# A state-space layer gated by a GLU: two full-row phases per chunk instead of three, and row statistics of the last chunk on ScalarE

## The chip, the cores and the metric

The kernel runs on one core of a Trainium2 chip. A core has a matrix engine (TensorE, "PE", with its weight loads listed as "PEld"), a vector engine (VectorE, "DVE"), an activation engine (ScalarE, "ACT"), a general engine (GpSimd, "POOL") and a queue that issues transfers (SyncE, "SP"). Each works through its own list of instructions in order and waits for the others by semaphores. The metric is the device time of one execution in microseconds. Beside it there is one profiled execution, whose trace has the start, the length and the releaser of every instruction.

## What is computed

The input `x` has 2048 rows (tokens) of 448 values. Each row is normalized; a diagonal complex recurrence runs along the rows; a gated two-layer network runs on each row; the two are multiplied and added to the input.

```python
x = A_x
xn = _layernorm(x, axis=-1)
s = _A_ref(xn, ...)            # recurrence with 448 complex states, then 2*Re(C h) + xn*Dskip
g = _silu(_B_ref(xn, ...))     # (sigmoid(xn w_gate) * (xn w_up)) w_down, 448 -> 1792 -> 448
return x + s * g

# inside _A_ref
Bu = jnp.einsum("bld,pd->blp", x + 0j, B_bar)
for t in range(L):
    h = Lam_bar[None, :] * h + Bu[:, t, :]
y = 2.0 * jnp.einsum("blp,dp->bld", hseq, Cmat).real + x * Dskip[None, None, :]
```

## The kernel before

The 2048 rows are cut into four chunks of 512 (`L`), and each chunk into four tiles of 128 rows. All matrix products of a chunk use `xnT`, the normalized rows transposed. The work of a chunk is:

- `stats` (line 421): mean and variance of one row tile, a `bn_stats` (L423) and a `bn_aggr` (L424) on DVE. `chain` (line 426) makes from them the factor and the offset of the normalization; for chunks 2 and 3 these are five small POOL instructions on two row tiles at a time (L437 to L446).
- `prepare(c)` (line 508): `norm` writes the normalized tile `xn` with one ACT pass (L456), POOL completes it (L459), two DMA transposes from SP's queue (L373) write it into `xnT`, and `skip_row` multiplies it by `Dskip` on DVE (L464). The `xnT` of chunk 2 lies on the memory of the raw C matrices, so that its transposes must stand behind `c_scale` (line 648), which makes the scaled C matrices `cT` from them (L656, L659, L666, L668).
- `gu_step(c, i)` (line 711): fourteen of them per chunk, seven column blocks, each a gate and an up product. A step is seven pairs of matmuls that use 64 rows of the array each, side by side (L690, L691); I call them half-row pairs. The gate's step is finished by a tanh pass on ACT (L704), the up step by a DVE instruction that writes `hF` (L707). The products use three PSUM buffers `gu`.
- `b_units(c, pts)` (line 733): the input of the recurrence, two of four column groups per call. It starts with half-row pairs (L743 to L748); the rest are full-row matmuls (L758, L761). Between the two the call can put other work (`mid`). ACT copies the result to `bus`.
- `whole(c)` (line 913): the recurrence of the chunk on DVE, three calls of `ssm_pair` and one of `ssm_stack`: rotate (L805, L806, L808), scan (L812, L844), rotate back into `hT` (L826, L827, L829). `hT` has two buffers, for even and odd chunks.
- `down(c, j)` (line 866): 14 full-row matmuls of one row tile (L873), followed by a silu pass on ACT into a buffer `g_t` (L879). `yout(c, j)` (line 884): 7 full-row matmuls with `cT` (L898), then three DVE instructions that add the skip row, multiply with `g_t` and add `x` (L904, L906, L908), and a store from SP (L910). Both take turns on two PSUM buffers `acc`.

The order is not written out engine by engine. The kernel adds operations with their inputs, outputs and an assumed cost to a plan (`Plan.add`, line 85). `Plan.solve` (line 138) keeps PE in the order in which its operations were added, works back from PE's times to the latest time of every other operation, and then lets each other engine take, among the operations that are ready, the one that is due first. So the end of the file, with its calls of `gu_step`, `b_units`, `down` and `yout`, is PE's order, and the lists of DVE, ACT, POOL and SP follow from it and from the assumed costs.

In chunks 1, 2 and 3 PE's order has three stretches of full-row work each: one that opens with `b_units(c, (0, 1))`, one with `b_units(c, (2, 3))`, and one of two `down` and two `yout` before the last two `gu_step`. Behind chunk 3 there is one more, up to the end. `down(c, ...)` runs in chunk c+1, and so do the first two `yout(c, ...)`; the last two run in chunk c+2.

Of the kernel before, what the change touches and what calls it, by code (L numbers as in the profile page):

```python
# [10 lines left out]
FP32 = mybir.dt.float32  # L11
BF16 = mybir.dt.bfloat16
I32 = mybir.dt.int32
ALU = mybir.AluOpType
ACT = mybir.ActivationFunctionType
# [3 lines left out]
D = 448  # L19
# [4 lines left out]
NT = S_TOK // P  # L24
# [4 lines left out]
EPS = 1e-5  # L29
# [44 lines left out]
class Plan:  # L74
# [10 lines left out]
    def add(self, eng, cost, fn, r=(), w=(), dma=0, lat=None, chain=False, name="", rate=230e3):  # L85
        o = Op()
        o.idx, o.eng, o.cost, o.fn, o.dma, o.name = len(self.ops), eng, cost, fn, dma, name
        o.lat = LAT.get(eng, 0.0) if lat is None else lat
        o.pre, o.suc, o.rate = {}, [], rate
        o.slot = None  # L90
        if dma and eng != "POOL":
            o.slot, self.n_dma = self.n_dma, self.n_dma + 1
        o.start = o.end = None
        for k in r:
            if k in self.w:
                self._edge(self.w[k], o, True)
        for k in w:
            for q in self.r.get(k, ()):
                self._edge(q, o, False)
            if k in self.w:  # L100
                self._edge(self.w[k], o, True)
        for k in w:
            self.w[k] = o
            self.r[k] = []
        for k in r:
            if k not in w:
                self.r.setdefault(k, []).append(o)
        if chain or eng == "PE" or (eng == "DVE" and self.seq):
            key = ("chain", eng)
            if key in self.last_of:  # L110
                self._edge(self.last_of[key], o, None)
            self.last_of[key] = o
        self.ops.append(o)
        return o
# [131 lines left out]
def kernel(  # L246
# [18 lines left out]
    V, A, G, T, Q = nc.vector, nc.scalar, nc.gpsimd, nc.tensor, nc.sync  # L265
# [5 lines left out]
    def sbt(name, shape, dt=BF16):  # L271
        return sb.tile([P] + list(shape), dt, name=name)
# [9 lines left out]
    x_all = sbt("x_all", [NT, D])  # L282
# [24 lines left out]
    iota = wv_raw[0][:].bitcast(FP32)  # L307
    NSIG = 2
    sig = [sbt(f"sig{i}", [2, L], FP32) for i in range(NSIG)]
    NGT, NO = 6, 3  # L310
    g_t = [sbt(f"g_t{i}", [D]) for i in range(NGT)]
    o_t = [sbt(f"o_t{i}", [D]) for i in range(NO)]
    ctmp = [sbt(f"ctmp{i}", [D], FP32) for i in range(2)]
# [8 lines left out]
    mv = sbt("mv", [NT, 2])  # L322
# [2 lines left out]
    veb = sbt("veb", [NT, 1])  # L325
    halfc, negc, expc = (sbt(n, [1], FP32) for n in ("halfc", "negc", "expc"))
    sdb = sbt("sdb", [NT, 1])
    rsd = sbt("rsd", [NT, 1], FP32)
    nmr = sbt("nmr", [NT, 1], FP32)
    col = {}  # L330
# [14 lines left out]
    add = pl.add  # L345
# [75 lines left out]
    def stats(t):  # L421
        b = t % 3
        add("DVE", 0.6, lambda: V.bn_stats(out=bst[b][:], in_=x_all[:, t, :]), r=[("x", t)], w=[("bst", b)])  # L423
        add("DVE", 0.16, lambda: V.bn_aggr(out=mv[:, t, :], in_=bst[b][:]), r=[("bst", b)], w=[("mv", t)])  # L424

    def chain(t0, n):
        ts = range(t0, t0 + n)
        var, mean = mv[:, t0:t0 + n, 1:2], mv[:, t0:t0 + n, 0:1]
        sd, rs, nm, ve = (q[:, t0:t0 + n, :] for q in (sdb, rsd, nmr, veb))
        ks = lambda k: [(k, t) for t in ts]  # L430
        if t0 < TPC:
            add("ACT", 0.3, lambda: A.activation(sd, var, ACT.Sqrt, bias=epsc[:]), r=ks("mv") + ["sqrttab", "epsc"], w=ks("sd"))
            add("POOL", 0.15, lambda: G.tensor_copy(out=meanf[:, t0:t0 + n, :], in_=mean), r=ks("mv"), w=ks("mf"))
            add("DVE", 0.2, lambda: V.reciprocal(out=rs, in_=sd), r=ks("sd"), w=ks("rs"))
            return
        bc = lambda t: t[:].unsqueeze(1).to_broadcast((P, n, 1))
        add("POOL", 0.4, lambda: G.tensor_single_scalar(out=ve, in_=var, scalar=EPS, op=ALU.add), r=ks("mv"), w=ks("ve"))  # L437
        add("POOL", 1.0, lambda: G.tensor_tensor(out=sd, in0=ve, in1=bc(halfc), op=ALU.pow), r=ks("ve") + ["consts"], w=ks("sd"))
        if t0 == TPC:
            add("DVE", 0.2, lambda: V.reciprocal(out=rs, in_=sd), r=ks("sd"), w=ks("rs"))  # L440
            add("DVE", 0.16, lambda: V.scalar_tensor_tensor(out=nm, in0=mean, scalar=-1.0, in1=rs, op0=ALU.mult, op1=ALU.mult),
                r=ks("mv") + ks("rs"), w=ks("nm"))
            return
        add("POOL", 1.0, lambda: G.tensor_tensor(out=rs, in0=sd, in1=bc(negc), op=ALU.pow), r=ks("sd") + ["consts"], w=ks("rs"))
        add("POOL", 0.4, lambda: G.tensor_tensor(out=nm, in0=mean, in1=rs, op=ALU.mult), r=ks("mv") + ks("rs"), w=ks("nm"))
        add("POOL", 0.4, lambda: G.tensor_single_scalar(out=nm, in_=nm, scalar=-1.0, op=ALU.mult), r=ks("nm"), w=ks("nm"))  # L446
# [58 lines left out]
    def gate(keys, key):  # L505
        add("NONE", 0.0, lambda: None, w=list(keys) + (key if isinstance(key, list) else [key]), lat=0.0)

    def prepare(c):
        if c == 2:
            gate([("rC", 0), ("rC", 1), ("rC3", 0), ("rC3", 1), "rC3l"], "xnT2free")  # L510
        for j in range(TPC):
            norm(c * TPC + j)
            dma_transpose(c * TPC + j)
            skip_row(c * TPC + j)
# [196 lines left out]
    def gu_step(c, i, first=False):  # L711
        m, k = (i // 2, "gu"[i % 2]) if c else (i % 7, "gu"[i // 7])
        a = next_gu()
        gu_mm(c, k, m, a, 0, TPC, first)
        gu_evac(c, k, m, a)
# [150 lines left out]
    def down(c, j, first=False, bank=None):  # L866
        key, d = bank if bank else (lambda a: (("acc", a), acc[a][:, 0:D]))(next_acc())
        js = slice(j * P, j * P + P)

        def f():  # L870
            for ft in range(FT):
                m, h = ft % 7, ft // 7
                T.matmul(d, lhsT=hF[c % 2][:, m, h, js], rhs=wd[:, ft, :], start=(ft == 0), stop=(ft == FT - 1))  # L873
        add("PE", 14 * 0.189 + (SW if first else 0), f, r=[("wd", 0), ("wd", 1)] + [("hF", c % 2, m) for m in range(7)], w=[key],
            name=f"d{c}.{j}")
        g = gt_n[0] % NGT
        gt_n[0] += 1
        gt_of[c, j] = g
        add("ACT", act(448), lambda: A.activation(g_t[g][:], d, ACT.Silu, scale=0.5), r=[key, "silutab"], w=[("gt", g)])  # L879
# [33 lines left out]
    def whole(c):  # L913
        if c < 2:
            gate([("nu" if c else "v", p) for p in range(4)], [("hT", c, p) for p in range(4)])
        for p in (0, 1):
            ssm_pair(c, p)
        ssm_stack(c)
        ssm_pair(c, 2)
# [31 lines left out]
    load_wd(0)  # L951
    def stats_for(c):
        for t in range(4 * c, 4 * c + 4):
            stats(t)
            if c > 1 and t % 2:
                chain(t - 1, 2)
        if c == 1:
            chain(4, 4)
# [23 lines left out]
    one(1, 0, "u")  # L982
    prepare(2)
    b_units(1, (0, 1), lambda: down(0, 0, True))
    for i in range(3, 6):
        gu_step(1, i, i == 3)
    b_units(1, (2, 3), lambda: down(0, 1, True))
    for i in range(6, 12):
        gu_step(1, i, i == 6)
    down(0, 2, True)  # L990
    yout(0, 0)
    down(0, 3)
    yout(0, 1)
    for i in range(12, 14):
        gu_step(1, i, i == 12)
    whole(1)

    for i in range(0, 4):
        gu_step(2, i)
    b_units(2, (0, 1), lambda: down(1, 0, True))  # L1000
    yout(0, 2)
    for i in range(4, 7):
        gu_step(2, i, i == 4)
    b_units(2, (2, 3), lambda: down(1, 1, True))
    yout(0, 3)
    prepare(3)
    for i in range(7, 12):
        gu_step(2, i, i == 7)
    down(1, 2, True)
    yout(1, 0)  # L1010
    down(1, 3)
    yout(1, 1)
    for i in range(12, 14):
        gu_step(2, i, i == 12)
    whole(2)

    for i in range(0, 4):
        gu_step(3, i)
    b_units(3, (0, 1), lambda: down(2, 0, True))
    yout(1, 2)  # L1020
    for i in range(4, 7):
        gu_step(3, i, i == 4)
    b_units(3, (2, 3), lambda: down(2, 1, True))
    yout(1, 3)
    for i in range(7, 12):
        gu_step(3, i, i == 7)
    down(2, 2, True)
    yout(2, 0)
    down(2, 3)
    yout(2, 1)  # L1030
    for i in range(12, 14):
        gu_step(3, i, i == 12)
    whole(3)

    yout(2, 2, True)
    yout(2, 3)
    free_banks = []
    for s in range(3):
        a = (gu_n[0] + s) % 3
        for i in range(2):  # L1040
            free_banks.append((("gub", a, i), gu[a][:, i, 0:D]))
        gate([("gu", a)], [("gub", a, 0), ("gub", a, 1)])
    for j in range(2):
        down(3, j, bank=free_banks[j])
    for j in range(2):
        yout(3, j)
    down(3, 2, bank=free_banks[2])
    yout(3, 2)
    down(3, 3, bank=free_banks[3])
    a = next_acc()  # L1050
    yout(3, 3, banks=[(("acc", a), acc[a]), free_banks[4]], parts=((0, 128), (128, 448)))
# [36 lines left out]
```

## Time and profile before

| | |
|---|---|
| median of 4 runs | 188.83 us (187.81 to 189.45) |
| profiled execution | 188.76 us |
| its span, first to last instruction | 186.9 us |
| granted clock of TensorE | 0.998 |
| DVE: `bn_stats` (L423), `bn_aggr` (L424) | 16 each, 613 and 166 ns |
| ACT: silu into `g_t` (L879), normalization (L456) | 540 and 755 ns |
| full-row matmuls of `down` and `yout` on 128x448 | 189 ns apart |
| half-row pairs on 512 columns | 215 ns apart |

The span is what the trace shows; the 1.9 us up to the time of the same execution lie around it. Durations of matmuls in the trace are longer than the distance of their starts, since they overlap in the array; the distance is what a matmul costs. A row of a group gives busy time, mean length and the idle time before it. The busy share of an engine is an average over stages with different limits.

### The profile page before, as it was taken

How to read it: one execution, taken by the hardware profiler on the slowest of the kernel's cores; microseconds unless marked ns; L12 is line 12 of the kernel's file. 1: busy time of each engine (PE TensorE's matmuls, PEld its weight loads, DVE VectorE, ACT ScalarE, POOL GpSimd, SP SyncE). 2: the span in 40 equal slices, each digit the busy share in tenths (PEclk: the TensorE clock that was granted, in tenths of full speed). 3: DMA queues.
4: the chain of work that ended last, by engine and by line, in shares of the span. 5: the costliest groups of instructions: out<-in, count | busy, mean ns of one | idle time of the engine just before them, and what ended most of it. 6: DMA issues, size and time to landing. Idle time of an engine off the chain costs nothing.

```text
span 186.9 us, 3512 instructions
## 1 busy us (share of the span) xinstructions
PE 180.4 (96%) x1375; PEld 87.7 (47%) x1375; DVE 167.9 (90%) x303; ACT 88.0 (47%) x124; POOL 35.0 (19%) x87
## 2 busy tenths in 40 slices
PE   7999998999999999999999999999999999999991
PEld 2584443474444444444445445444445445445550
DVE  3832999999998899999999999999999999999963
ACT  3549997953949942241567441324444421501020
POOL 7134351920078100000037410000000000000000
PEclk9999999999999999999999999999999999999999
DMA  5999999399100035200000343000000000001220
GB/s 133 278 213 229 186 212 171 75 263 232 61 4 0 0 76 65 59 0 4 0 2 0 77 102 70 0 28 0 25 4 0 25 25 28 0 2 51 74 77 25
DMA packets 30257, 13.43 MB, mean 72 GB/s; under 512 B 19744, under 2 KB 30240, under 8 KB 30240
## 3 DMA queue, kind: packets, MB, share of 16 engines
q1 hardware_dynamic: 28336, 12.05, 31.0%
q10 hardware_dynamic: 1808, 1.15, 2.3%
q8 instruction: 11, 0.18, 0.4%
q14 instruction: 6, 0.05, 0.1%
q0 software_dynamic: 96, 0.00, 0.0%
HBM read 6.77 MB, written 1.84 MB: 46 GB/s over the span
## 4 chain that ended last, share of the span: by engine, by line
PE 60%; DVE 21%; DMA 8%; ACT 4%; issue 3%; POOL 1%; SPq 1%; DVEq 0%
PE gu L690 24%; PE acc L873 13%; PE acc L898 10%; PE gu L873 6%; DMA x_all<-in_A_x_dram 5%; DVE hF L707 4%; PE gu L758 4%; DMA wG<-in_B_w_gate_dram 3%; DVE wv L812 3%; DVE bst L423 2%; DVE cT L659 1%; DVE ta L805 1%; DVE ta L826 1%; SPq L351 1%; DVE tb L806 1%
## 5 line engine op out<-in xcount | busy, mean ns | idle before, releaser
L690 PE MATMUL gu<-xnT,wG 64*128 64x512 bf16 (+1 forms) x231 | 46.2, 344 | 0.3 <-DVE xnT L491 0.3
L691 PE MATMUL gu<-xnT,wG 64*128 64x512 bf16 (+1 forms) x231 | 46.2, 344 | 0.0
L690 PE MATMUL gu<-xnT,wU 64*128 64x512 bf16 x196 | 46.0, 376 | 0.0
L691 PE MATMUL gu<-xnT,wU 64*128 64x512 bf16 x196 | 46.0, 376 | 0.0
L704 ACT ACTIVATE sig<-gu 128x1024 f32<-128x1024 f32 x21 | 21.4, 1024 | 28.6 <-PE gu L691 24.2
L873 PE MATMUL acc<-wd,hF 128*128 128x448 bf16 x168 | 33.8, 353 | 0.2 <-ACT g_t L879 0.2
L873 PEld LDWEIGHTS <-hF 128*128 128x128 bf16 x224 | 21.2, 98 | 22.6 <-issue 3.9
L690 PEld LDWEIGHTS <-wG 64*128 64x128 bf16 x231 | 21.0, 94 | 21.3 <-issue 2.1
L690 PEld LDWEIGHTS <-wU 64*128 64x128 bf16 x196 | 18.1, 94 | 23.3 <-issue 1.4
L707 DVE SCALAR_TENSOR_TENSOR hF<-sig,gu 128x1024 bf16<-128x1024 f32 x21 | 25.5, 1212 | 2.5 <-PE gu L691 1.3
L812 DVE TENSOR_TENSOR_SCAN wv<-c_r,st,z 128x512 bf16<-128x512 f32 x18 | 23.0, 1275 | 0.0
L898 PE MATMUL acc<-cT,hT 128*128 128x448 bf16 (+1 forms) x112 | 22.6, 344 | 0.0
L691 PEld LDWEIGHTS <-wG 64*128 64x128 bf16 x231 | 20.9, 94 | 0.0
L879 ACT ACTIVATE g_t<-acc 128x448 bf16<-128x448 f32 x12 | 6.5, 540 | 28.5 <-PE acc L873 28.5
L691 PEld LDWEIGHTS <-wU 64*128 64x128 bf16 x196 | 18.1, 94 | 0.1
L758 PE MATMUL gu<-xnT,bT 128*128 128x512 bf16 x72 | 16.9, 379 | 0.0
L423 DVE BATCH_NORM_STATS2 bst<-x_all 128x6 f32<-128x448 bf16 x16 | 9.4, 613 | 7.8 <-DMA x_all<-in_A_x_dram 7.8
L898 PEld LDWEIGHTS <-hT 128*128 128x128 bf16 x119 | 11.3, 98 | 10.0 <-issue 0.4
L769 ACT CAST bus<-gu 128x1024 bf16<-128x1024 f32 x12 | 12.0, 1004 | 2.9 <-PE gu L758 2.8
L456 ACT ACTIVATE xn<-x_all,nmr,rsd 128x448 bf16<-128x448 bf16 x12 | 8.8, 755 | 7.3 <-DVE xd L464 4.6
L873 PE MATMUL gu<-wd,hF 128*128 128x448 bf16 x56 | 11.1, 352 | 0.0
L904 DVE TENSOR_TENSOR o_t<-acc,xd 128x448 bf16<-128x448 f32 (+1 forms) x16 | 9.5, 594 | 1.5 <-PE acc L898 1.4
(135 smaller groups left out, 239.3 us busy)
## 6 DMA issues: line engine op xcount, KB each, us to landing
out_dram<-o_t SPq DMA_DIRECT2D x15, 112.0 KB, 1.7
wd<-in_B_w_down_dram SPq DMA_DIRECT2D x2, 784.0 KB, 5.1
x_all<-in_A_x_dram SPq DMA_DIRECT2D x3, 448.0 KB, 4.8
wU<-in_B_w_up_dram SPq DMA_DIRECT2D x2, 448.0 KB, 11.6
wU<-in_B_w_up_dram SPq DMA_DIRECT2D x2, 336.0 KB, 6.9
wG<-in_B_w_gate_dram SPq DMA_DIRECT2D x2, 224.0 KB, 5.9
wG<-in_B_w_gate_dram ACTq DMA_DIRECT2D x2, 224.0 KB, 5.9
xnT<-xn SPq DMA_TRANSPOSE x24, 2.4
```

What stands on the lines that cost most here:

```text
L423: add("DVE", 0.6, lambda: V.bn_stats(out=bst[b][:], in_=x_all[:, t, :]), r=[("x", t)], w=[("bst", b)])
L456: add("ACT", 0.65, lambda: A.activation(xn[b][:, 0:448], x_all[:, t, :], ACT.Identity, bias=nmr[:, t, :], scale=rsd[:, t, :]), r=[("x", t) ...
L690: T.matmul(gu[a][:, 0, ts], lhsT=w_[0:H, s, ms], rhs=x[0:H, s, ts], start=(s == 0), stop=(s == 6))
L691: T.matmul(gu[a][:, 1, ts], lhsT=w_[H:P, (s + 1) % 7, ms], rhs=x[H:P, s, ts], start=(s == 0), stop=(s == 6))
L704: add("ACT", act(1024), lambda: A.activation(th, gu[a][:], ACT.Tanh, scale=0.5), r=[("gu", a)], w=[tk])
L707: add("DVE", dve1(1024), lambda: V.scalar_tensor_tensor(out=ho, in0=th, scalar=1.0, in1=gu[a][:], op0=ALU.add, op1=ALU.mult), r=[("gu", a) ...
L758: T.matmul(gu[a][:, i, :], lhsT=bT[:, kt, i, pt * P:pt * P + P], rhs=x[:, 2 * kt, :], start=False, stop=(kt == 2))
L769: add("ACT", act(1024), lambda u=u, a=a: A.copy(out=bus[u][:], in_=gu[a][:]), r=[("gu", a)], w=[("bus", u)])
L812: dve(1.194, lambda k=k: V.tensor_tensor_scan(out=wv[:, k, :], data0=rb, data1=z[:, k, :], initial=(st[pt][:, k, :] if c else 0.0), op0=AL ...
L873: T.matmul(d, lhsT=hF[c % 2][:, m, h, js], rhs=wd[:, ft, :], start=(ft == 0), stop=(ft == FT - 1))
L898: T.matmul(y, lhsT=hT[c % 2][:, hm, js], rhs=cT[:, cm, c0:c1], start=(i == 0), stop=(i == 6))
L904: add("DVE", dve1(n), lambda od=od, y=y, c0=c0, c1=c1: V.tensor_tensor(out=od, in0=y, in1=xq[:, c0:c1], op=ALU.add), r=[key, ("xd", q)], w ...
```

## The change

Three things change. The calls at the end of the file are put in another order: each of chunks 1, 2 and 3 has two full-row stretches, each with two `down` and, in chunks 2 and 3, two `yout`, all four of which now belong to chunk c-2; the tail has four `yout(2, ...)` in place of two, and its own order. The mean and the variance of the four row tiles of chunk 3 come from ACT: one Identity pass whose accumulated output is the row's sum, then one Square pass, with minus the mean as its bias, whose accumulated output is the sum of squares; three POOL instructions per two tiles scale them. And there are small edits: one `g_t` buffer fewer, four new small tiles, and higher assumed costs for two POOL operations in `chain`, which the planner uses.

```diff
-    NGT, NO = 6, 3
+    NGT, NO = 5, 3
...
+    junk = sbt("junk", [D])
+    smf, nmf, sqf = (sbt(n, [NT, 1], FP32) for n in ("smf", "nmf", "sqf"))
...
+    def act_stats(t0):
+        sm, nf, sq, me, va = (q[:, t0:t0 + 2, :] for q in (smf, nmf, sqf, mv[:, :, 0:1], mv[:, :, 1:2]))
+        ts = (t0, t0 + 1)
+        for t in ts:
+            add("ACT", 0.62, lambda t=t: A.activation(junk[:], x_all[:, t, :], ACT.Identity, accum_out=smf[:, t, :]),
+                r=[("x", t), "silutab"], w=[("sm", t), "junk"])
+        add("POOL", 0.4, lambda: G.tensor_single_scalar(out=nf, in_=sm, scalar=-1.0 / D, op=ALU.mult),
+            r=[("sm", t) for t in ts], w=[("nf", t) for t in ts])
+        add("POOL", 0.4, lambda: G.tensor_single_scalar(out=me, in_=sm, scalar=1.0 / D, op=ALU.mult),
+            r=[("sm", t) for t in ts], w=[("me", t) for t in ts])
+        for t in ts:
+            add("ACT", 0.62, lambda t=t: A.activation(junk[:], x_all[:, t, :], ACT.Square, bias=nmf[:, t, :],
+                                                      accum_out=sqf[:, t, :]),
+                r=[("x", t), ("nf", t)], w=[("sq", t), "junk"])
+        add("POOL", 0.4, lambda: G.tensor_single_scalar(out=va, in_=sq, scalar=1.0 / D, op=ALU.mult),
+            r=[("sq", t) for t in ts] + [("me", t) for t in ts], w=[("mv", t) for t in ts])
...
-        add("POOL", 0.4, lambda: G.tensor_single_scalar(out=ve, in_=var, scalar=EPS, op=ALU.add), r=ks("mv"), w=ks("ve"))
-        add("POOL", 1.0, lambda: G.tensor_tensor(out=sd, in0=ve, in1=bc(halfc), op=ALU.pow), r=ks("ve") + ["consts"], w=ks("sd"))
+        add("POOL", 0.6, lambda: G.tensor_single_scalar(out=ve, in_=var, scalar=EPS, op=ALU.add), r=ks("mv"), w=ks("ve"))
+        add("POOL", 1.4 if n == 4 else 1.0, lambda: G.tensor_tensor(out=sd, in0=ve, in1=bc(halfc), op=ALU.pow), r=ks("ve") + ["consts"], w=ks("sd"))
...
     def stats_for(c):
         for t in range(4 * c, 4 * c + 4):
-            stats(t)
+            if c not in (3,):
+                stats(t)
+            elif t % 2:
+                act_stats(t - 1)
...
     b_units(1, (0, 1), lambda: down(0, 0, True))
+    down(0, 1)
     for i in range(3, 6):
         gu_step(1, i, i == 3)
-    b_units(1, (2, 3), lambda: down(0, 1, True))
-    for i in range(6, 12):
+    b_units(1, (2, 3), lambda: down(0, 2, True))
+    down(0, 3)
+    for i in range(6, 14):
         gu_step(1, i, i == 6)
-    down(0, 2, True)
-    yout(0, 0)
-    down(0, 3)
-    yout(0, 1)
-    for i in range(12, 14):
-        gu_step(1, i, i == 12)
     whole(1)
...
+    for c in (2, 3):
+        for i in range(0, 4):
+            gu_step(c, i)
+        b_units(c, (0, 1), lambda: down(c - 1, 0, True))
+        yout(c - 2, 0)
+        down(c - 1, 1)
+        yout(c - 2, 1)
+        for i in range(4, 7):
+            gu_step(c, i, i == 4)
+        b_units(c, (2, 3), lambda: down(c - 1, 2, True))
+        yout(c - 2, 2)
+        down(c - 1, 3)
+        yout(c - 2, 3)
+        if c == 2:
+            prepare(3)
+        for i in range(7, 14):
+            gu_step(c, i, i == 7)
+        whole(c)
+
+    yout(2, 0, True)
     yout(2, 1)
...
-    yout(2, 2, True)
-    yout(2, 3)
...
-    for j in range(2):
-        down(3, j, bank=free_banks[j])
-    for j in range(2):
+    down(3, 0, bank=free_banks[0])
+    yout(2, 2)
+    down(3, 1, bank=free_banks[1])
+    yout(2, 3)
+    down(3, 2, bank=free_banks[2])
+    for j in range(3):
         yout(3, j)
-    down(3, 2, bank=free_banks[2])
-    yout(3, 2)
     down(3, 3, bank=free_banks[3])
```

The calls of chunks 2 and 3 that stood in the place of the loop are left out.

More of the change, by code (lines that the diff above doesn't have):

```diff
@@ L984 @@
     b_units(1, (0, 1), lambda: down(0, 0, True))
+    down(0, 1)
     for i in range(3, 6):
         gu_step(1, i, i == 3)
-    b_units(1, (2, 3), lambda: down(0, 1, True))
-    for i in range(6, 12):
+    b_units(1, (2, 3), lambda: down(0, 2, True))
+    down(0, 3)
+    for i in range(6, 14):
         gu_step(1, i, i == 6)
-    down(0, 2, True)
-    yout(0, 0)
-    down(0, 3)
-    yout(0, 1)
-    for i in range(12, 14):
-        gu_step(1, i, i == 12)
-    whole(1)
[L998 to L1029, printed above, removed]
-    yout(2, 1)
-    for i in range(12, 14):
-        gu_step(3, i, i == 12)
-    whole(3)
-    yout(2, 2, True)
-    yout(2, 3)
+    whole(1)
+    for c in (2, 3):
[17 more added lines that the diff above has]
+    yout(2, 0, True)
+    yout(2, 1)
     free_banks = []
```

## Prediction

> **What bounds the kernel now.** I read the busy shares first, then the tenths by slice, because a mean share hides stages with different limits.
>
> ```profile
> PE 180.4 (96%) x1375; PEld 87.7 (47%) x1375; DVE 167.9 (90%) x303; ACT 88.0 (47%) x124; POOL 35.0 (19%) x87
> ```
>
> ```profile
> PE   7999998999999999999999999999999999999991
> ...
> DVE  3832999999998899999999999999999999999963
> ```
>
> TensorE works from the first slice to the last but one. VectorE's 90% is an average over an idle start, an idle end and a middle with almost no room. The table of windows puts numbers on the middle (columns: stretch, length, then busy time of each engine, granted clock, DMA share, GB/s):
>
> ```profile
> 20.00:60.00 40.00, 39.26 (x328) 19.06 (x326) 39.30 (x70) 30.23 (x48) 17.26 (x38) 1.00 0.68 134
> 60.00:100.00 40.00, 39.77 (x290) 18.23 (x287) 38.47 (x65) 17.75 (x24) 4.74 (x11) 1.00 0.14 24
> 100.00:145.00 45.00, 45.00 (x327) 21.32 (x325) 44.36 (x75) 19.52 (x26) 5.21 (x9) 1.00 0.13 32
> 145.00:165.00 20.00, 20.00 (x147) 9.14 (x146) 19.53 (x33) 6.47 (x9) 0.00 (x0) 1.00 0.05 18
> 165.00:183.00 18.00, 17.85 (x102) 9.39 (x99) 15.77 (x37) 2.07 (x4) 0.00 (x0) 1.00 0.16 53
> ```
>
> Both PE and DVE are full from 20 to 165 us, and ACT is half empty from 60 us on. Which of the two full engines sets the end is told by the waits of PE:
>
> ```profile
> PE gu L417 <- DVE hF L376: 1.2, 1, 1.2
> PE gu L743 <- DVE hF L707: 0.7, 1, 0.7
> PE gu L690 <- DVE xnT L491: 0.3, 1, 0.3
> PE acc L873 <- ACT g_t L879: 0.2, 1, 0.2
> ```
>
> That is 2.4 us in the whole span; the first three lie before 31 us (start, first transposes, and L743 at 30.27), the last at 70.95. So PE sets the end, and DVE keeps up with it without room. PE also runs at its pace: 14 matmuls of a `down` take 2.65 us in the chain (189 ns each), 7 of a `yout` 1.32. A change can win only matmul time, switches between matmul forms, or those few waits. The price of a switch stands in PE's timeline around one full-row phase:
>
> ```profile
> 109.65 0.38 PE L690 MATMUL gu<-xnT,wU 64*128 64x512 bf16 x1
> ...
> 109.96 2.82 PE L873 MATMUL acc<-wd,hF 128*128 128x448 bf16 x14
> 112.62 1.49 PE L898 MATMUL acc<-cT,hT 128*128 128x448 bf16 x7
> 113.94 2.81 PE L873 MATMUL acc<-wd,hF 128*128 128x448 bf16 x14
> 116.59 1.49 PE L898 MATMUL acc<-cT,hT 128*128 128x448 bf16 x7
> 118.01 0.39 PE L690 MATMUL gu<-xnT,wG 64*128 64x512 bf16 x1
> 118.02 0.39 PE L691 MATMUL gu<-xnT,wG 64*128 64x512 bf16 x1
> 118.24 0.38 PE L690 MATMUL gu<-xnT,wG 64*128 64x512 bf16 x1
> ```
>
> Starts of half-row pairs are 0.215 apart inside a step. Here the last one and the first full-row matmul are 0.31 apart (+0.095). The first `yout` takes 1.32 up to the next start, the second 1.42 (+0.10), and the first half-row pitch is 0.23 (+0.015). A phase costs 0.21 us.
>
> One more row matters, the weight loads' wait for a transposed chunk, with the queue that carries the transposes:
>
> ```profile
> 78.27 0.09 PEld L690 LDWEIGHTS <-wG 64*128 64x128 bf16 x1 [0.34 <-DMA xnT<-xn]
> ```
>
> ```profile
> 65.64 11.42 SPq L373 DMA_TRANSPOSE xnT<-xn  x8
> ```
>
> The eight transposes of chunk 2 land with no slack at all where chunk 2 begins (78.05). They leave SP's queue one behind the other from 65.64, right after the last `cT` instruction of DVE (L668, 64.89 plus 0.70), since chunk 2's `xnT` lies on the raw C matrices that `c_scale` reads.
>
> **The change part by part.**
>
> *Phases.* Chunks 1, 2 and 3 have three full-row phases each before, two each after; the last phase, behind chunk 3, stays. Three phases go: 3 x 0.21 = 0.63 us off PE. The Trainium skill (TensorEngine Tiling (Array Packing), Key Properties) says that changing the tiling mode drains TensorE. A full drain would let the last half-row matmul's whole record, 0.376, pass before the next start: 0.16 above the pitch, and 6 switches would give 0.97. The trace shows less than that both ways; I take 0.63.
>
> *`yout` moved later.* Two of each chunk's four `yout` move to the next chunk, and two more `yout(2)` into the tail. Matmuls are the same in number and form: 0 on PE in sum. Their DVE work (594 + 369 + 371 ns) and their stores on SP move with them; 15 of 16 stores are full rows of 1.7 us to landing and none is waited for by an engine before the end. What moves is the time at which chunk 2 begins: 2 x 1.32 + 0.21 earlier, plus the 0.23 wait at 70.95 if it goes: 78.05 becomes about 75.0. Everything due there must be 3.1 us earlier: `c_scale`, four norms, the POOL copies and the eight transposes. Against that, the scan of chunk 0, which had to be ready at 69.2 for `yout(0,0)`, is now due at about 87 (75.0, four gate/up steps of 1.51, the half-row pairs 0.43, `down` 2.75, B products 2.6). On DVE, between 53 and 69 us, scans (L844, L812) and rotations (L826, L827, L829, L858) of chunk 0 and chunk 1 stand among the `cT` instructions; that work, over 8 us, can give way, and the order is computed from due times. I take 0 for the transposes; the other end is 3.1.
>
> *Wait at 70.95.* PE waits there 0.23 for a `g_t` pass that stood behind a norm on ACT. The same `down` comes elsewhere now: minus 0.23, or 0 if another pass stands in its way. I take minus 0.23.
>
> *Row statistics.* DVE loses 4 x (613 + 166) = 3.1 us between 88 and 100 us. ACT gets eight passes; nearest rows are 540 ns (L879, no pointer operand) and 755 (L456, two): about 0.56 for Identity and 0.65 for Square, 4.8 us. The accumulated sum may take an instruction of its own; the trace has none, its smallest ACT instruction is 192 ns, so 0 to 1.6 us for eight; I take 1.6: 6.4 us on ACT. The Trainium skill (ScalarE: Activation LUTs, Rules for kernel authors) speaks against this part: adds and multiplies belong on VectorE, per element up to about three times faster. By that rule alone the change pays 6.4 for 3.1 and should lose 3.3 us; by the windows ACT works 17.75 of 40 us where DVE works 38.47, so the passes cost the end nothing, provided that they sit past 60 us or in gaps. Where they don't, as between 55.7 and 63.8, where ACT was busy without a gap and DVE once waited 1.0 us for it, one pass of 0.75 delays a gate evacuation by that much, and three `gu` buffers cover about two steps of 1.5. Value 0, other end 0.75 per misplaced pass.
>
> If Square were not in the resident function table, each pair would load twice: 4 x 1283 ns, the duration of the table load in the trace. The same page (Table sets) says cheap functions sit in every set as filler. No run here shows it; value 0. POOL gets six small instructions (200 to 1110 ns in the rows of L437 and L446), ahead of a chain that had the same inputs at 92 to 100 us and whose result is wanted at 103.8: ACT's sums can come 20 us before. Queued behind them on POOL are the copies that complete `xn` for the transposes; cover some 10 us, then 0.3 to 1 us each.
>
> *Small edits.* One `g_t` buffer fewer makes `down(1,1)`'s pass wait for the product of `yout(0,0)`: 0.6 + 0.37 on DVE against 2.65 of matmuls, cover 1.6 us. The planner's dearer POOL costs change only the order. Between a gain of 0.74 (PE's wait at 30.27 for L707 goes, because the tables that stand before it are less urgent with chunk 0's scan) and a like loss I take 0.
>
> *The tail.* `yout(3,0)` starts at 172.24, the last `hT` write ends at 171.22: 1.0 us of slack. After the change the tail starts at 164.19 - 2.64 - 0.63 - 0.23 = 160.7, and four `yout` and three `down` (13.2) stand before `yout(3,0)`: 173.9. DVE gets 1.7 us more and has 3.1 less to do. Three `yout` then follow each other on two `acc` banks: the third waits unless DVE frees the first within 1.32. DVE needs 0.6; 0, or 0.5 if it lags as at 176.07 (1.2 behind). The end behind PE stays, 4.0 us from 182.88.
>
> **Sum**: -0.63 - 0.23 = -0.86 us. The profiled execution took 188.76 for a span of 186.9, and the median of the runs is 188.83, as good as equal. So 187.9 to 188.0.
>
> **The rivals.**
>
> *Slower: transposes late.* If `c_scale` still ends at 65.6, PE arrives at 75.0 and waits until 78.1: 3.1 us, paid for at once and not regained by an engine that has no other gaps. 188.8 - 0.9 + 3.1 = 191.0. For it: the queue is full from 65.64 to 77.06 and lands with zero slack; four us of full ACT (55.7 to 63.8) stand before the last two ACT passes of `c_scale`. Against it: the last two pairs of `cT` before them (58.20, 58.77) had their ACT input at 53.2 and waited only for their turn. It decides from the point where L668 ends later than 62.5; each us past it costs one.
>
> *Faster: DVE's room is worth more.* The 0.74 at 30.27 and the 0.3 at 7.57 go as well: 188.8 - 0.9 - 1.0 = 186.9. Against it: both lie before any statistic is moved.
>
> *ACT or POOL in the way.* Two or three sum passes land in the full stretch and hold a gate evacuation; 1 to 2 us of PE waits: 189 to 190.
>
> *No effect of fewer phases.* The B products begin with half-row pairs, so the phase opens as before; only the third phase goes. If switching were hidden, 188.6.
>
> **How the numbers follow.** Forecast without a new wait (187.4 to 188.5) 0.57; no effect (188.5 to 188.9) 0.06; faster rival (186.7 to 187.4) 0.10; transposes late, in part or in full (189 to 191.2) 0.16; ACT, POOL or an order that fits worse (188.9 to 192) 0.11. One per cent, about what a measurement here tells from no change, is 1.9 us: 186.9 and 190.7. Faster than that needs nearly all of PE's removable waits: 0.06. Slower takes most of the transposes' case and half of the last one, and some allowance for an order computed anew: 0.22. Range 186.8 to 191.1.
>
> **What would show it.** PE's starts: 0.31 and 0.23 at two phases per chunk, no third; chunk 2's first matmul at about 75.0 with no wait of PE for `xnT`; L668 before 62.5 and the first transpose of eight right behind. DVE's busy time 164.8, ACT's about 94. The tail starts near 160.7. A row of PE waiting for `xnT` or for an L879 or L704 pass of over 1 us, or added table loads, would make me wrong.

## The result, and the profile after

The changed kernel takes 187.48 us (median of 32 runs, 186.77 to 189.23); the kernel before took 188.33 us in 51 runs beside it. The ratio is 0.995 with a 95% interval of 0.9935 to 0.9965: 0.85 us less on the medians (0.7 to 1.2 by the interval), clear of no change and well under one per cent. The profiled execution took 187.46 us for a span of 185.6, where the one before had 188.76 and 186.9. These two traces are 1.3 us apart, more than the medians are; single executions of either kernel spread by over 1 us, so the ratio gives the size and the traces give the places.

The busy shares and the tenths by slice of the changed kernel come first:

```profile
PE 179.8 (97%) x1375; PEld 89.0 (48%) x1375; DVE 165.7 (89%) x295; ACT 93.0 (50%) x140; POOL 38.5 (21%) x93
```

```profile
PE   7999999999999999999999999999999999999991
...
DVE  3731999999989899999999999899999999999763
```

DVE has eight instructions less and is busy 2.2 us less, ACT has sixteen more and is busy 5.0 us more, and the number of matmuls is the same. The lengths of the eight instructions add up to 3.1 us and those of the sixteen to 6.5; busy time is less than such a sum where neighbours overlap in the trace. PE is still the engine without a gap. The table of windows of the changed kernel has the same columns as before:

```profile
20.00:60.00 40.00, 39.73 (x322) 20.10 (x319) 39.05 (x70) 33.01 (x57) 18.96 (x44) 1.00 0.71 137
60.00:100.00 40.00, 40.00 (x303) 18.50 (x302) 39.29 (x64) 22.65 (x35) 10.74 (x19) 1.00 0.15 32
100.00:145.00 45.00, 45.00 (x327) 21.58 (x326) 43.65 (x72) 17.27 (x23) 1.18 (x1) 1.00 0.08 21
```

ACT rises to 33.01 of 40 us in the first stretch, so part of the sums did go where ACT had little room. DVE is busy 0.7 us less between 100 and 145 and is otherwise as full as it was. The waits of PE show what that did:

```profile
PE gu L419 <- DVE hF L378: 1.2, 1, 1.2
PE gu L709 <- DVE xnT L510: 0.3, 1, 0.3
PE gu L765 <- ACT sig L723: 0.3, 1, 0.3
```

The waits of 0.74 at 30 us and 0.23 at 71 us are gone. The first one was for two `hF` writes of DVE (L707). DVE's timeline before them, in the kernel before:

```profile
26.77 0.75 DVE L562 SCALAR_TENSOR_TENSOR hT<-hT,hT 128x513 f32<-128x513 f32 x1
...
27.86 2.35 DVE L707 SCALAR_TENSOR_TENSOR hF<-hF,gu 128x1024 bf16<-128x1024 bf16 x2
30.13 0.69 DVE L562 SCALAR_TENSOR_TENSOR hT<-hT,hT 128x513 f32<-128x513 f32 x1
```

and in the changed kernel:

```profile
27.15 2.34 DVE L726 SCALAR_TENSOR_TENSOR hF<-hF,gu 128x1024 bf16<-128x1024 bf16 x2
29.41 1.29 DVE L581 SCALAR_TENSOR_TENSOR hT<-hT,hT 128x513 f32<-128x513 f32 x2
```

L562 (L581 after) is one of the steps that make the sine and cosine tables of the recurrence; it runs four times. The third stood ahead of the two writes, and they ended at 30.21; now the third and the fourth stand behind them, and they end at 29.49.

A new wait of 0.27 stands at 54.90, for a tanh pass (L723). ACT's timeline there says why:

```profile
52.01 0.53 ACT L898 ACTIVATE g_t<-acc 128x448 bf16<-128x448 f32 x1
52.57 0.58 ACT L432 ACTIVATE junk<-x_all 128x448 bf16<-128x448 bf16 x1
53.05 0.18 ACT L432 ACTIVATION_READ_ACCUMULATOR junk<-x_all 128x1 f32 x1
53.27 0.58 ACT L432 ACTIVATE junk<-x_all 128x448 bf16<-128x448 bf16 x1
53.75 0.18 ACT L432 ACTIVATION_READ_ACCUMULATOR junk<-x_all 128x1 f32 x1
53.84 1.00 ACT L723 ACTIVATE sig<-gu 128x1024 f32<-128x1024 f32 x1
```

Two of the eight sums run in front of the tanh pass that frees the next PSUM buffer. A sum is two instructions, the pass and a read of the accumulator; the second one starts 0.70 us after the first, and the plan had counted 0.62. From start to start PE loses 0.43 us here.

One full-row phase of the changed kernel, in PE's timeline (columns: start, length, engine, line, operation; x14 is one `down`, x7 one `yout`):

```profile
96.74 2.82 PE L892 MATMUL acc<-wd,hF 128*128 128x448 bf16 x14
99.40 1.46 PE L777 MATMUL gu<-xnT,bT 128*128 128x512 bf16 x6
100.70 0.82 PE L780 MATMUL gu<-xnT,bT 128*128 128x256 bf16 x6
101.35 1.49 PE L917 MATMUL acc<-cT,hT 128*128 128x448 bf16 x7
102.68 2.81 PE L892 MATMUL acc<-wd,hF 128*128 128x448 bf16 x14
105.33 1.49 PE L917 MATMUL acc<-cT,hT 128*128 128x448 bf16 x7
106.75 0.39 PE L709 MATMUL gu<-xnT,wU 64*128 64x512 bf16 x1
```

It holds two `down`, two B products and two `yout`, with one exit to half-row work (1.42 instead of 1.32 after the last `yout`). SP's queue with the eight transposes of chunk 2:

```profile
57.54 11.15 SPq L375 DMA_TRANSPOSE xnT<-xn  x8
```

They start 8.1 us earlier than before. The last issue is over at 68.69; PE's first matmul of chunk 2 starts at 74.57, 5.9 us later, and its weight loads show no wait.

### The profile page after: what moved, and what is told of

Its sections match the earlier page's. It is cut to its first block, busy times and chain, and to the rows that moved or that the text cites. A ratio compares the mean times of both kernels' runs of the same rounds, so it can differ in the third digit from the quotient of the medians.

```text
span 185.6 us, 3527 instructions
## 1 busy us (share of the span) xinstructions
PE 179.8 (97%) x1375; PEld 89.0 (48%) x1375; DVE 165.7 (89%) x295; ACT 93.0 (50%) x140; POOL 38.5 (21%) x93
## 4 chain that ended last, share of the span: by engine, by line
PE 68%; DVE 14%; DMA 8%; ACT 4%; issue 2%; SPq 1%; DVEq 0%
PE gu L709 29%; PE acc L892 15%; PE acc L917 11%; PE gu L892 6%; DMA x_all<-in_A_x_dram 5%; PE gu L777 5%; DVE hF L726 4%; DMA wG<-in_B_w_gate_dram 3%; DVE wv L831 2%; DVE hT L581 1%; DVE bst L425 1%; ACT ctmp L675 1%; DVE ta L824 1%; PE gu L780 1%; DVE tb L825 1%
## 5 line engine op out<-in xcount | busy, mean ns | idle before, releaser
L723 ACT ACTIVATE sig<-gu 128x1024 f32<-128x1024 f32 x21 | 21.3, 1021 | 30.3 <-PE gu L710 27.9
L709 PEld LDWEIGHTS <-wG 64*128 64x128 bf16 x231 | 21.3, 94 | 20.7 <-issue 1.9
L726 DVE SCALAR_TENSOR_TENSOR hF<-sig,gu 128x1024 bf16<-128x1024 f32 x21 | 25.4, 1211 | 1.9 <-PE gu L710 1.5
L710 PEld LDWEIGHTS <-wG 64*128 64x128 bf16 x231 | 21.2, 94 | 0.0
L425 DVE BATCH_NORM_STATS2 bst<-x_all 128x6 f32<-128x448 bf16 x12 | 7.0, 611 | 7.6 <-DMA x_all<-in_A_x_dram 7.6
L788 ACT CAST bus<-gu 128x1024 bf16<-128x1024 f32 x12 | 12.0, 1004 | 2.3 <-PE gu L777 2.3
L478 POOL COPY xn<-xn 128x64 bf16<-128x64 bf16 x12 | 5.8, 487 | 29.1 <-ACT xn L475 29.0
L898 ACT ACTIVATE g_t<-gu 128x448 bf16<-128x448 f32 x4 | 2.2, 543 | 18.8 <-PE gu L892 18.8
```

Source lines behind the costliest of these rows:

```text
L709: T.matmul(gu[a][:, 0, ts], lhsT=w_[0:H, s, ms], rhs=x[0:H, s, ts], start=(s == 0), stop=(s == 6))
L710: T.matmul(gu[a][:, 1, ts], lhsT=w_[H:P, (s + 1) % 7, ms], rhs=x[H:P, s, ts], start=(s == 0), stop=(s == 6))
L723: add("ACT", act(1024), lambda: A.activation(th, gu[a][:], ACT.Tanh, scale=0.5), r=[("gu", a)], w=[tk])
L726: add("DVE", dve1(1024), lambda: V.scalar_tensor_tensor(out=ho, in0=th, scalar=1.0, in1=gu[a][:], op0=ALU.add, op1=ALU.mult), r=[("gu", a) ...
L788: add("ACT", act(1024), lambda u=u, a=a: A.copy(out=bus[u][:], in_=gu[a][:]), r=[("gu", a)], w=[("bus", u)])
```

## The experiments

Twelve kernels ran, two of them without an edit. The theories: **(1)** the gain is the three phases of 0.21 us and the waits of PE that come and go with the new order; **(2)** the phases are hidden and the work taken off DVE moves the end. Each ratio is to runs of the kernel before on the same chip.

| kernel | median, us | ratio | 95% interval |
|---|---|---|---|
| change, again | 187.39 | 0.9934 | 0.9903 to 0.9965 |
| phases only | 187.85 | 0.9970 | 0.9948 to 0.9992 |
| sums only | 189.41 | 1.0040 | 1.0014 to 1.0067 |
| change with old POOL costs | 188.03 | 0.9974 | 0.9957 to 0.9990 |
| POOL costs only | 188.23 | 0.9984 | 0.9961 to 1.0007 |
| phases only, old POOL costs | 188.53 | 0.9995 | 0.9967 to 1.0023 |
| third phase back, ordered | 187.75 | 0.9966 | 0.9946 to 0.9986 |
| sums at their true cost | 187.21 | 0.9925 | 0.9897 to 0.9953 |
| sums later | 187.21 | 0.9924 | 0.9891 to 0.9957 |
| transposes late | 187.48 | 0.9948 | 0.9927 to 0.9969 |
| before, again | 188.40 | 0.9995 | 0.9973 to 1.0017 |

**The change, again.** No edit.

> The changed kernel itself, on the same chip as the three that take it apart. Both theories: 0.7 to 1.2 us below the kernel before; PE waits 0.3 us for the ACT tanh pass near 55 us and nowhere else after 8 us.

1.06 us below the kernel before. PE's wait near 55 us is smaller in this trace and is not listed: the two starts are 0.24 us further apart than normal, against 0.43 in the first trace. The size of that wait differs between executions.

**Phases only.** In the changed kernel, whose POOL costs and five `g_t` buffers stay:

```diff
-            if c not in (3,):
-                stats(t)
-            elif t % 2:
-                act_stats(t - 1)
+            stats(t)
```

> The two phases per chunk, with the row statistics of chunk 3 left on DVE (bn_stats, bn_aggr as before). Theory 1 (three phases of 0.21 us and the waits of PE that go with the new order are the whole gain): 0.6 to 1.1 us below the kernel before, so the same as the changed kernel or up to 0.3 us better, since the 0.3 us wait for a tanh pass behind the sums goes. Theory 2 (the phases are hidden, the 3.1 us taken off DVE are what moves the end): 0 to 1 us above the kernel before, with waits of PE for DVE.

0.6 us below, at the lower edge of theory 1 and clear of no change, with no wait of PE listed after its first 8.2 us. DVE kept all its work, so theory 2 falls: relief of DVE is not needed for the gain. The spans of these runs have a median about 1.0 us below those of the kernel before (185.7 and 186.7). In 7 of the 22 runs more than 2.2 us lie outside the span, in none of the 52 of the kernel before; no trace shows where that time goes.

The traces show one thing that the sums add. PE's three `yout` of the tail, in the changed kernel and then here:

```profile
173.44 4.13 PE L917 MATMUL acc<-cT,hT 128*128 128x448 bf16 x21
```

```profile
173.34 4.36 PE L917 MATMUL acc<-cT,hT 128*128 128x448 bf16 x21
```

The last `hT` write of DVE that they need, in the same order:

```profile
169.18 0.68 DVE L848 TENSOR_TENSOR hT<-ta,tb 128x1024 bf16<-128x1024 bf16 x1
```

```profile
172.07 0.68 DVE L848 TENSOR_TENSOR hT<-ta,tb 128x1024 bf16<-128x1024 bf16 x1
```

With the statistics on DVE it comes to the tail 2.9 us later, the third `yout` is held up by 0.23 us, and DVE ends later behind PE. From its first matmul to the end of the span the tail takes 25.8 us here and in the other trace with the phases alone, and 25.3 to 25.4 in the eight traces with the sums. So in the new order the sums are worth 0.4 us at the end and cost up to 0.4 near 55 us. In whole runs they can't be told from nothing: the intervals of this kernel and of the change overlap.

**Sums only.** In the kernel before, `act_stats` and its tiles put in, called as in the change, five `g_t` buffers.

> The kernel before with only the row statistics of chunk 3 on ACT (and five g_t buffers); three phases per chunk. Theory 1: within 0.4 us of the kernel before, DVE busy 3.1 us less, PE's busy time unchanged at 180.4. Theory 2: 0.7 to 0.9 us below the kernel before.

About 0.75 us above the kernel before by the ratio (1.0040; the medians are 0.96 apart), more than either theory expected. In its trace PE waits 0.99 us at 71.40 for a `g_t` pass, where the kernel before waits 0.23:

```profile
71.40 2.81 PE L892 MATMUL acc<-wd,hF 128*128 128x448 bf16 x14 [0.99 <-ACT g_t L898]
```

ACT's timeline in front of it:

```profile
68.20 0.75 ACT L475 ACTIVATE xn<-x_all,nmr,rsd 128x448 bf16<-128x448 bf16 x1
70.16 0.67 ACT L439 ACTIVATE junk<-x_all,nmf 128x448 bf16<-128x448 bf16 x1 [1.21 <-POOL nmf L434]
70.74 0.19 ACT L439 ACTIVATION_READ_ACCUMULATOR junk<-x_all,nmf 128x1 f32 x1
70.83 0.52 ACT L898 ACTIVATE g_t<-acc 128x448 bf16<-128x448 f32 x1
```

The Square pass waits 1.21 us for minus the mean (`nmf`), which POOL computes, and POOL's timeline shows the power operations of the same two-tile chains in front of it:

```profile
67.30 1.01 POOL L457 TENSOR_TENSOR sdb<-veb,halfc 128x2 bf16<-128x2 bf16 x1
68.40 1.23 POOL L463 TENSOR_TENSOR rsd<-sdb,negc 128x2 f32<-128x2 bf16 x1
69.59 0.23 POOL L478 COPY xn<-xn 128x64 bf16<-128x64 bf16 x1
69.91 0.22 POOL L434 TENSOR_SCALAR nmf<-smf 128x2 f32<-128x2 f32 x1
```

Behind the waiting Square stands the silu of the `down` whose PSUM buffer PE needs. In the old order a `down` and a `yout` alternate there, with two buffers. In the changed order that stretch of chunk 1 holds gate and up steps alone; there the last two Squares run at 68.23 and 69.01, and the tanh pass behind them waits for PE, not PE for it. So the sums are paid for in the old order, and the new order makes room for them.

The wait at 30 us is absent from this trace, for a reason of that execution: the table step still stands ahead of the two `hF` writes (26.50), but PE comes 0.46 us later than in the kernel before, because its transposes at the start took longer, and the writes end 0.30 earlier. Behind that place PE is 0.31 ahead of the kernel before, behind the wait at 71.40 it is 0.45 late: that wait costs 0.75.

**Old POOL costs in the change, and the POOL costs alone.** In the changed kernel, and the reverse in the kernel before:

```diff
-        add("POOL", 0.6, lambda: G.tensor_single_scalar(out=ve, ...
-        add("POOL", 1.4 if n == 4 else 1.0, lambda: G.tensor_tensor(out=sd, ...
+        add("POOL", 0.4, lambda: G.tensor_single_scalar(out=ve, ...
+        add("POOL", 1.0, lambda: G.tensor_tensor(out=sd, ...
```

> The changed kernel with the planner's two POOL costs as they were before (0.4 and 1.0). If these costs are what removed PE's wait of 0.74 us near 30 us, it comes back and the time is 0.5 to 0.8 us above the changed kernel. If it went because chunk 0's scan is due later, the time and PE's waits stay those of the changed kernel within 0.3 us.

> The kernel before with only the planner's POOL costs changed (0.6, and 1.4 for four tiles). The order of PE is the same, so its busy time stays 180.4. If the costs are a gain of their own, as the run with the old ones suggests, the time is 0.4 to 0.7 us below the kernel before; if they only matter beside the new order of PE, no difference (within 0.3).

With the old costs the change takes 0.64 us more (188.03 against 187.39 on the same chip), though the intervals still touch. The trace has a wait of 0.49 us for a bus copy of ACT (L788) that comes late behind the table work of chunk 0:

```profile
33.32 0.27 PE L765 MATMUL gu<-xnT,bT 64*128 64x256 bf16 x1 [0.49 <-ACT bus L788]
```

It is a different wait from the one at 30 us, which has not come back, so these costs are not what removed that one. Alone, the costs give a difference that its interval doesn't tell from none; PE's waits are only redistributed (0.41 at 24.79 and 0.40 at 30.34 in place of one of 0.74).

**Phases only, with the old POOL costs.** Both edits above together.

> The two phases per chunk alone: statistics on DVE, old POOL costs. By the switches and the wait at 71 us: 0.63 to 0.86 us below the kernel before, if no wait is new. If the old costs bring a wait near 33 us here too, as they did beside the sums, 0.1 to 0.4 below.

Inconclusive. The trace has no wait of PE over 0.2 us after the first 8 us, and its span is 185.7, as a gain would have it. But of the 14 runs only 5 have such spans (185.6 to 185.8), the other 9 have 186.3 to 187.3; their median time is that of the kernel before (188.53 against 188.47), and the interval holds both no gain and 0.6 us. What holds up its longer executions is in no trace. So the new order alone isn't shown to be faster in whole runs; with the new costs it is.

**The third phase back.** In the changed kernel:

```diff
-        down(c - 1, 3)
-        yout(c - 2, 3)
-        if c == 2:
-            prepare(3)
-        for i in range(7, 14):
+        for i in range(7, 12):
             gu_step(c, i, i == 7)
+        down(c - 1, 3, True)
+        yout(c - 2, 3)
+        if c == 2:
+            prepare(3)
+        for i in range(12, 14):
+            gu_step(c, i, i == 12)
```

and the same for `down(0, 3)` in chunk 1. A first form (187.98 us, 0.9974) left `prepare(3)` in front of the moved `yout(0, 3)`, so that this one tile was computed with the skip row of another; the work is the same.

> The changed kernel with a third full-row phase opened again in chunks 1, 2 and 3: down 3 (with yout 3 in chunks 2 and 3) moves from the second phase to a place before the last two gate/up steps. Nothing else moves. Theory 1: three more phases of 0.21, so 0.6 us above the changed kernel, PE's busy time up by 0.6. Theory 2: no difference, since DVE's load is the same.

> As the third phase put back, with the preparation of chunk 3 kept behind the last yout of chunk 0, so that no skip row is written over before it is read and the whole computation is done. By the switches alone: 0.6 us above the changed kernel.

0.36 us above the change on medians of two different chips, and the intervals of the two kernels overlap. The traces say where the rest is. Counted from the first gate matmul, the tail starts at 152.43 in the ordered form and at 152.05 in the second trace of the change. The extra phases cost +0.21 in chunk 1, +0.22 in chunk 2, +0.21 in chunk 3, and the wait of 0.25 at the B products of chunk 1, which the change itself has, is absent here: 0.64 - 0.25 = 0.39. One such phase in the timeline of the ordered form:

```profile
109.93 0.38 PE L710 MATMUL gu<-xnT,wU 64*128 64x512 bf16 x1
110.24 2.82 PE L892 MATMUL acc<-wd,hF 128*128 128x448 bf16 x14
112.89 1.49 PE L917 MATMUL acc<-cT,hT 128*128 128x448 bf16 x7
114.31 0.39 PE L709 MATMUL gu<-xnT,wG 64*128 64x512 bf16 x1
...
114.54 0.38 PE L709 MATMUL gu<-xnT,wG 64*128 64x512 bf16 x1
```

0.31 on the way in, 1.42 on the way out and 0.23 after it, as in the kernel before. The price of a phase is shown in the traces; the times agree with it but don't prove it.

**Sums at their true cost, and sums later.** In the changed kernel. The first has the two costs alone; the second has them, the added input `("bus", 2, 2)`, and its call of `stats_for(3)` behind the second B products of chunk 1:

```diff
-            add("ACT", 0.62, lambda t=t: A.activation(junk[:], x_all[:, t, :], ACT.Identity, ...
-                r=[("x", t), "silutab"], ...
+            add("ACT", 0.70, lambda t=t: A.activation(junk[:], x_all[:, t, :], ACT.Identity, ...
+                r=[("x", t), "silutab", ("bus", 2, 2)], ...
...
-                add("ACT", 0.62, ... ACT.Square, ...
+                add("ACT", 0.78, ... ACT.Square, ...
```

> The changed kernel with the planner told what the two sum passes take in its trace from start to start, 0.70 and 0.78 us, in place of 0.62. If PE's wait of 0.3 us near 55 us comes from sum passes that run longer than planned in front of a tanh pass, it goes: 0.2 to 0.4 us below the changed kernel. If the plan has no freedom there, no difference.

> As the one before, and the plan holds the sum passes back until the bus copies of chunk 1 (about 63 us), past the stretch in which ACT has no gap. If sums in that stretch cost anything, PE has no wait after 8 us and the time is 0.2 to 0.5 us below the changed kernel; if not, no difference.

Both 187.21 us, and in both traces PE's wait near 55 us is gone. Told the true cost, the plan puts one sum in front of that tanh pass instead of two (the second moves to 56.39). By the ratios, which allow for the chips, they are 0.2 to 0.5 us below the two measurements of the change, by about what the trace's wait is worth, but the intervals overlap. They are clearly faster than the kernel before, and no slower than the change.

**Transposes late.** In the changed kernel:

```diff
+        def f():
+            for _ in range(TWICE.get(keys[0], 1)):
+                Q.dma_start_transpose(out=o, in_=i)
-        add("SP", 1.2, lambda: Q.dma_start_transpose(out=o, in_=i), ...
+        add("SP", 1.2, f, ...
...
+    TWICE = {("xnT", 2, 0, "a"): 2, ("xnT", 2, 0, "b"): 2}
```

> The changed kernel with the two transposes of chunk 2's first row tile issued twice (the same data again), unknown to the plan, so that the other six start later. In the changed kernel the last of the eight lands near 70 us and PE wants it at 74.6: 4.6 us of slack. Each repeat adds 1.2 us, or up to 3.6 if it waits for the transfer it repeats. If slack is what kept this rival from happening, the delay is 2.5 us with no effect, or 7 us with a wait of PE of about 2.5 us for xnT at the start of chunk 2 and a time up by as much.

The time is that of the change. SP's queue holds the transposes 5.1 us longer than the 11.15 of the change, 2.5 for each repeat:

```profile
58.72 16.25 SPq L379 DMA_TRANSPOSE xnT<-xn  x10
```

The last issue is over at 74.97 and PE comes to chunk 2 at 75.76: of the 5.9 us between the two in the change 0.8 are left. The second pair of matmuls there starts 0.22 late, and the profile names no releaser for it. A delay of 5.1 us used the slack up and cost next to nothing. This trace is the longest of the kernel's 20 runs (188.67 us) for another reason:

```profile
56.09 0.27 PE L770 MATMUL gu<-xnT,bT 64*128 64x256 bf16 x1 [1.44 <-ACT sig L728]
```

ACT had waited 1.57 us at 46.71 for the transfer of the C matrices and ran over 1 us behind from there, and the two sums stood once more in front of the tanh pass. So the delay that makes the rival real was reached only at its edge; a larger one wasn't tried.

**The kernel before, again.** No edit.

> The kernel before, unchanged, for a second trace. If PE's waits of 0.74 us at 30 us and 0.23 at 71 us belong to the kernel and not to that one execution, both are there again, and the time is that of the kernel before.

Both waits are there again (0.74 at 30.63, 0.24 at 71.33). They belong to the kernel, and the table step stands ahead of the two `hF` writes as in the first trace.

## Why the prediction was right

It said 188.0 us, 0.86 below the 188.83 of the kernel before that it started from; measured are 187.48, 0.85 below the 188.33 that more runs of the kernel before gave. The two terms that it counted are there, but the match is in good part luck, because three terms that it took as 0 were not. Point by point:

- **Phases, -0.63.** Right in size and kind: in the traces 0.21 to 0.22 for each one put back. The full drain of the prediction's estimate (0.97) would have been too much.
- **The wait at 71 us, -0.23.** Gone in both traces of the change.
- **The wait at 30 us, taken as 0.** It went, -0.74, the whole of the favourable end, and for the reason given there: in all nine kernels that ran with PE's new order the third table step stands behind the two `hF` writes, whatever the POOL costs and wherever the statistics are; in the three with the old order it stands ahead. That a later due time of chunk 0's scan is what moved it is the prediction's reading of the planner and wasn't tested by itself.
- **The sums, taken as 0.** Right in sum, not in its parts: up to 0.4 lost at 54.90, where 0.75 for each misplaced pass was the bound given, and 0.4 won in the tail, which the prediction didn't count. The cost on ACT was well sized: 577 and 661 ns for the passes (0.56 and 0.65 forecast), 187 to 190 on average for each read of the accumulator (192 taken). There is no added table load, two in the traces before and after; the section that the prediction cites for this (Trainium skill, ScalarE: Activation LUTs, Table sets) names relu, copy, identity and abs as fillers, not Square, so for Square it is the trace that shows it. The windows were right against the rule that the prediction quotes from the same page, for this order of PE; for the old order sums alone lose 0.75 us. The forecasts of busy time mixed lengths with busy time: DVE is at 165.7 (164.8 forecast), ACT at 93.0 (94).
- **POOL costs, taken as 0 ("change only the order").** The term that may be off most in whole runs. With the old ones in the changed kernel PE waits 0.49 at another place, and the median is 0.64 higher; the intervals touch.
- **Transposes, taken as 0.** Right. The last `cT` instruction ends at 57.4 (62.5 was the limit). DVE's rotations and scans gave way as read from the trace, and 5.9 us stood between the last issue and PE's arrival where there had been no slack.
- **The tail.** PE starts it at 160.19 (160.7 forecast) and `yout(3,0)` at 173.44 (173.9).

The terms of the traces, as the profile lists the waits, are -0.63 - 0.23 - 0.74 + 0.27 = -1.33. From start to start the same places give -0.63 for the phases, -0.40 at 71 us, -0.93 at 30 us and +0.43 at 55 us, and the first gate product stands 0.22 later: -1.31, against 1.29 between the two profiled spans. The medians are only 0.85 apart. What takes up the rest is not in these two traces; in 5 of the 32 runs of the change over 2.2 us lie outside the span. So the number was met because a wait of 0.74 that was not counted stands against the new wait, the late start and the spread between executions. In whole runs no single part carries the gain: the phases with the old costs and the costs alone each can't be told from no change, together they give 0.6.

## What to carry to other kernels

Where the matrix engine has no gaps, price each change of matmul form from the distances of starts in its timeline; that gain is small and can be read in advance, but the new order also moves the waits for the other engines, here by more than the gain itself. Work that moves to a half-idle engine is free on PE only if nothing urgent stands behind it in that engine's order, and a pass that waits for a third engine (here a Square that waits for POOL) holds up everything behind it. When a planner orders the engines, an assumed cost that is 0.1 us too low can put an urgent pass behind two others; costs read from the trace may be worth as much as a structural edit (here 0.2 to 0.6 us, with intervals that overlap).

## What was not expected of the hardware

A sum on ScalarE is two instructions in the trace: the pass (577 ns for Identity, 661 for Square with a bias operand) and a read of the accumulator (median 186 ns). The profiled execution of the phases with old costs took 188.69 us for a span of 185.7, 3.0 us outside the span, where the median of every kernel here is 1.8 to 2.0; a single time can thus be a microsecond off without any engine being slower.
